# One generator per sum block, the fourth hidden tile last, pauses of the background work, and 40 cut products in a planned fp32 kernel

## The chip, the core and the metric

The kernel runs on one core of a Trainium2 chip. The metric is the device time of one execution in microseconds (us). TensorE is PE in the profile (PEld is its weight load), VectorE is DVE, ScalarE is ACT, GpSimd is POOL, and SyncE, which issues the DMAs here, is SP.

## The reference

Three stages follow each other. All arrays are float32; the weights arrive as float64 and are converted on the chip.

```python
scores = cap * tanh((q @ k.T) / sqrt(64) / cap)       # 4 batches, 12 heads, 448 x 448, head 64
attn = softmax(scores); x = attn @ v                   # x as 1792 tokens x 768
y = (sigmoid(x @ w_gate) * (x @ w_val)) @ w_out        # 768 -> 1536 -> 768
h = y @ w_in2;  out = (h * cos(h)) @ w_out2            # 768 -> 2048 -> 768
```

## The kernel before, in words

Precision: every operand of a large product is split into a high part (rounded to fp32r) and a low part (the rest), and a product is three matmuls: high x high, high x low, low x high. The rounding is an ACT cast (`wh`, `x`, `gh`, `zh`), the rest a subtraction on DVE or POOL (`wl`, `x` again, `gl`, `zl`).

The tokens are worked on in two halves of 896 (two batches). After the attention PE does, in this order: the gate and value products of half 0, done plainly (`gate_value_plain`), its result (`result(0, ...)`), the gate and value products of half 1 in pairs (`gate_value_pairs`), its result (`result(1, ...)`), and then the second block of weights, first for half 1 and then for half 0 (`cosine`). In the paired stages two output tiles of 128 rows by 896 columns are made from seven block products instead of eight: `pair_products` runs products 1, 2, 6, 5, 7, 4, 3 over KH = 3 inner tiles, 63 matmuls of 448 columns, and `pair_sums` (L827, L836) adds them up out of PSUM. The first pair of a stage goes by rows: all seven products of inner tile 0, then of 1, then of 2. The operands of the seven products are sums and differences of input blocks; `block_sums` makes them, for x1 (tile `x1r`), y1 (tile `y`) and y0. In the kernel before one generator makes them in a fixed sequence; of each block the high part is cast on L1059 and the low part is a small spawned generator on L1065.

`cosine` follows the list `cd`: C pairs (hidden tiles of w_in2) and D groups (`out_group`): C0 C1 C2 D0 C3 C4 D1 C5 C6 C7 D2 D3. A D group multiplies four hidden tiles (GRP = 4, indices kk 0 to 3) by w_out2, for two halves of 384 columns (nb) and seven token tiles t. `hidden` makes h * cos(h) of one hidden tile in seven steps over ACT and DVE (L1171, L1176, L1179, L1188, L1190, L1193 for `zh`, L1196 for `zl`).

PSUM has eight banks; a pair uses seven of them, each token tile t of a D group one until `out_evict` has copied or added it out.

What sets the order of every engine is a planner that runs when the program is built: `Order` holds one generator per activity and always emits the operation that could start earliest by its own table of costs, plus a penalty of the generator (`pen`; H_PEN for `hidden`, W_PEN for weights, S_PEN for `pair_sums`). `get` and `get_w` give buffers under limits (the W_ ranges, `room`). The engines then run their queues strictly in that order. Beside the main line the background (`bg`, `bg_loads`) converts the 32 weight units of the last stage from float64 and writes them to DRAM (`kept`), one unit for each BG_STEP of planned PE time from BG_FROM on; `bg_go` is its gate. The splits of the gated tiles (`g_split`, L945 and L948) make the operands of `result`.

`mm3` and `mm3s` emit the matmuls of one product; both have a parameter `cut`, which is 0 everywhere in the kernel before:

```python
cuts = (0, cut, S) if cut and (wi, xi) == (0, 1) else (0, S)
for s0, s1 in zip(cuts, cuts[1:]):
    nc.tensor.matmul(b.ap[:, c, s0:s1], lhsT=w.part(wi, o, P), rhs=x[xi][:, s0:s1], ...)
```

Of the kernel before, what the change touches and what calls it, by code (L numbers as in the profile page):

```python
# [14 lines left out]
P = 128  # L15
# [218 lines left out]
def softcap_attention_gated_mlp_cos_mlp(  # L234
# [14 lines left out]
    nc = tc.nc  # L249
# [7 lines left out]
    KH = KD // 2  # L257
# [9 lines left out]
    NMID, NBIG = 49, 5  # L267
    F_AHEAD = 2
    H_PEN, S_PEN = 0.4, 0.0
    LEAD, AHEAD = 99, 4  # L270
    BG_PEN, BG_RAW, BG_ROOM = 1.0, 2, 2
# [3 lines left out]
    G_SPARE = 1, 6  # L275
# [69 lines left out]
    W_A0, W_B0, W_A1, W_B1, W_CD = (7, 14), (7, 14), (14, 18), (8, 14), (12, 16)  # L345
# [249 lines left out]
    def bg_go():  # L595
        return sch.free["PE"] > BG_FROM + bg_made[0] * BG_STEP
# [147 lines left out]
    def plain_product(w, x, kks, b, first, last):  # L744
        for i, kk in enumerate(kks):
            f, l = first and i == 0, last and i == len(kks) - 1
            if x[kk] is None:
# [3 lines left out]
                lambda kk=kk, f=f, l=l: mm3(b, w, kk, x[kk], f, l),  # L751
# [24 lines left out]
    def product(i, b, c, g, X, js, last_use):  # L776
# [3 lines left out]
        for j in js:  # L780
            if not X.ready(i, j):
# [3 lines left out]
                lambda j=j: mm3s(b, c, w, o + j * P, X.part(i, j), j == 0, j == KH - 1),  # L785
# [170 lines left out]
    def gate_value_plain(hf, x, ph):  # L956
        for m in range(KF):
            wg = yield from take(ph, ("g", m))
            pg = yield from bank(2)
            yield from plain_product(wg, x, range(KD), pg, True, True)  # L960
# [39 lines left out]
    def gate_value_pairs(X):  # L1000
        for p in range(KF // 2):
            yield from pair_products(("pair", "g", p), X, False, GateSink(p), p == 0)
            yield from pair_products(("pair", "v", p), X, p == KF // 2 - 1, ValueSink(p))

    def result(hf, ph, order, sink):
        for n, m in enumerate(order):
            if n == KD - 1 and hf == 0:
                done.add("again")
            pb = yield from bank(2)
            for s in range(2):  # L1010
                w = yield from take(ph, ("o", m, s))
                for kk in range(KF // 2):
# [4 lines left out]
                    yield from plain_product(w, x, [kk], pb, i == 0, i == KF - 1)  # L1017
# [38 lines left out]
    def block_split(X, i, j, src, o, c, room):  # L1056
        t = yield from get("x", F32R, room)
        X.t[i, j] = t
        yield act(S, lambda: nc.scalar.copy(out=at(t, 0, S), in_=at(src, o, S)), [c], [t.cell("h")])  # L1059
        spawn(block_low(t, src, o, c), wpen, "blow")  # L1060

    def block_low(t, src, o, c):
# [7 lines left out]
        src.free()  # L1070

    def block_sums(X, raw, room):

        e = {}
# [11 lines left out]
        def direct(j, i):  # L1086
            r, c = {1: (raw[j], 0), 2: (raw[j + KH], 0), 3: (raw[j + KH], 1)}[i]
            yield from block_split(X, i, j, r, c * S, r.cell(c), room)
# [9 lines left out]
        def later(j, i):  # L1098
            r0, r1 = raw[j], raw[j + KH]
            if i == 7:  # L1100
                yield tt(r0, S, r1, S, r0, S, [r1.cell(1), r0.cell(1)], [r0.cell(1)])
                yield from block_split(X, 7, j, r0, S, r0.cell(1), room)
            elif i == 4:
                yield lambda: X.t[2, j].cell("l").ok
                yield tt(r1, 0, r1, 0, e[j], S, [r1.cell(0), e[j].cell(1)], [r1.cell(0)])
                e[j].free()
                yield from block_split(X, 4, j, r1, 0, r1.cell(0), room)
            else:
                o = {6: S, 5: 0}[i]
                yield from block_split(X, i, j, e[j], o, e[j].cell(o // S), room)  # L1110
# [5 lines left out]
        for j in range(KH):  # L1116
            yield from steps(j)
            yield from direct(j, 1)
# [656 lines left out]
```

## Time and profile before

| what | value |
|---|---|
| time, median of 3 runs | 1196.14 us (1195.59 to 1196.61) |
| the profiled execution | 1195.84 us, its span 1194.0 us |
| PE busy | 1159.2 us, 97% of the span |
| DVE busy | 913.1 us, 76% |
| ACT busy | 668.6 us, 56% |
| POOL busy | 258.6 us, 22% |
| mean granted TensorE clock | 0.992 |

The span is the time between the first and the last recorded instruction; 1.84 us of the profiled execution lie outside it. An engine's busy time is the time in which at least one of its instructions was on record; matmuls overlap each other in it. In us from the span's start the attention's last matmul starts at 237, the paired gate and value products run from 475 to 638, the second result follows to 733, and the paired hidden tiles and the D groups to 1190. In the rows below L715 are the matmuls of plain products, L727 those of paired products, L1255 those of the D groups.

### The profile page before, as it was taken

The numbers are of one execution on the slowest core, as the hardware profiler recorded it, in microseconds if no ns is written. First come the engines' busy times: TensorE is split into PE (matmuls) and PEld (weight loads), VectorE is DVE, ScalarE is ACT, GpSimd is POOL, SyncE is SP. The second block draws the span as 40 slices with busy tenths as digits, with TensorE's granted clock in tenths as the row PEclk, the third lists the DMA queues.
The fourth block names the chain that finished last, engine by engine and source line by source line (L and its number), as shares of the span: only waits on it lengthen the run. The fifth ranks groups of instructions, "written<-read, shape, count | busy, mean of one in ns | idle before, by whom it ended". The sixth has DMA issues, their size and how long they took to land.

```text
span 1194.0 us, 15877 instructions
## 1 busy us (share of the span) xinstructions
PE 1159.2 (97%) x6090; PEld 989.7 (83%) x6090; DVE 913.1 (76%) x1127; ACT 668.6 (56%) x785; POOL 258.6 (22%) x140
## 2 busy tenths in 40 slices
PE   8999899999999999899998999999999998999998
PEld 4444455599999999799997998899999998999998
DVE  6999999698987876787778857837578877375862
ACT  6979788865655655433346534846356256452720
POOL 3766544400011000122211000302023312011300
PEclk9999999999999999899999999999999998999999
DMA  7424244477776775323235752203025231111303
GB/s 182 113 64 97 63 122 107 131 232 257 256 255 196 229 251 185 123 101 110 93 102 182 247 172 66 80 14 93 27 69 184 82 109 35 54 53 40 93 1 93
DMA packets 126187, 148.16 MB, mean 124 GB/s; under 512 B 49952, under 2 KB 98976, under 8 KB 126112
## 3 DMA queue, kind: packets, MB, share of 16 engines
q1 hardware_dynamic: 125824, 147.09, 39.9%
q8 instruction: 48, 0.79, 0.3%
q14 instruction: 27, 0.22, 0.1%
q10 hardware_dynamic: 288, 0.07, 0.0%
HBM read 112.13 MB, written 35.00 MB: 123 GB/s over the span
## 4 chain that ended last, share of the span: by engine, by line
PE 88%; DVE 7%; ACT 2%; issue 1%; SPq 0%; DMA 0%; DVEq 0%; ACTq 0%
PE pt L727 30%; PE pt L715 28%; PE pt L1255 19%; PE pt L1420 5%; PE pt L1395 4%; DVE r L1614 1%; ACT p L1486 1%; PE pt L1374 1%; PE pt L1441 1%; ACT p L1503 1%; DVE sum L1593 1%; DVE gl L948 1%; DVE zl L1196 1%; DVE h L827 0%; SPq L1329 0%
## 5 line engine op out<-in xcount | busy, mean ns | idle before, releaser
L727 PE MATMUL pt<-x,wh 128*128 128x448 f32 x1260 | 344.6, 369 | 7.1 <-DVE x L1065 3.7
L727 PEld LDWEIGHTS pt<-x,wh 128*128 128x128 f32 x1260 | 237.7, 189 | 31.5 <-DVE x L1065 4.4
L727 PE MATMUL pt<-x,wl 128*128 128x448 f32 x504 | 185.7, 368 | 0.0
L490 ACT CAST wh<-f 128x768 fp32r<-128x768 f32 (+1 forms) x164 | 122.9, 776 | 92.6 <-DVE f L655 50.3
L501 POOL TENSOR_TENSOR wl<-f,wh 128x768 fp32r<-128x768 f32 x41 | 80.1, 1957 | 381.8 <-ACT wh L490 297.3
L1255 PE MATMUL pt<-wh,zh 128*128 128x384 f32 x448 | 151.7, 339 | 6.1 <-ACT zh L1193 6.1
L1255 PE MATMUL pt<-wh,zl 128*128 128x384 f32 x448 | 151.9, 339 | 2.3 <-DVE zl L1196 2.3
L1255 PE MATMUL pt<-wl,zh 128*128 128x384 f32 x448 | 151.2, 337 | 0.0
L501 DVE TENSOR_TENSOR wl<-f,wh 128x768 fp32r<-128x768 f32 x95 | 96.8, 1024 | 45.9 <-ACT wh L490 45.6
L1486 ACT ACTIVATE p<-pt,tanh_scale 112x896 f32<-112x896 f32 x96 | 92.6, 1008 | 37.3 <-PE pt L1395 35.6
L727 PEld LDWEIGHTS pt<-x,wl 128*128 128x128 f32 x504 | 95.0, 188 | 9.3
L1278 DVE TENSOR_TENSOR acc<-pt,acc 128x384 f32<-128x384 f32 x84 | 46.6, 555 | 65.0 <-PE pt L1255 64.3
L1255 PEld LDWEIGHTS pt<-wh,zh 128*128 128x128 f32 x448 | 85.5, 191 | 6.8 <-ACT zh L1193 6.7
L1255 PEld LDWEIGHTS pt<-wh,zl 128*128 128x128 f32 x448 | 85.3, 190 | 3.8 <-DVE zl L1196 3.8
L1503 ACT ACTIVATE p<-p,cap_sb 112x1792 f32<-112x1792 f32 x48 | 86.2, 1795 | 0.0
L1255 PEld LDWEIGHTS pt<-wl,zh 128*128 128x128 f32 x448 | 85.4, 191 | 0.1
L715 PE MATMUL pt<-gl,wh 128*128 128x448 f32 x276 | 79.4, 369 | 4.1 <-DVE gl L948 4.1
L715 PE MATMUL pt<-xh,wh 128*128 128x448 f32 x288 | 83.4, 371 | 0.0
L715 PE MATMUL pt<-xl,wh 128*128 128x448 f32 x288 | 81.8, 365 | 0.0
L715 PE MATMUL pt<-xh,wl 128*128 128x448 f32 x288 | 81.8, 365 | 0.0
L1420 PE MATMUL pt<-p,v 112*64 112x448 f32 x384 | 77.5, 545 | 4.2 <-ACT p L1486 4.2
L1395 PEld LDWEIGHTS pt<-qs,ks 64*112 64x112 f32 x576 | 46.2, 171 | 41.9 <-ACT p L1486 16.7
(121 smaller groups left out, 2075.3 us busy)
## 6 DMA issues: line engine op xcount, KB each, us to landing
f<-kept SPq DMA_DIRECT2D x100, 384.0 KB, 3.5
kept<-f SPq DMA_DIRECT2D x36, 384.0 KB, 3.4
braw<-in_moe_w_in_dram SPq DMA_DIRECT2D x16, 768.0 KB, 5.5
kept<-bf SPq DMA_DIRECT2D x32, 384.0 KB, 2.7
braw<-in_moe_w_out_dram SPq DMA_DIRECT2D x16, 768.0 KB, 6.1
raw<-in_moe_w_gate_dram SPq DMA_DIRECT2D x12, 768.0 KB, 5.1
raw<-in_moe_w_val_dram SPq DMA_DIRECT2D x12, 768.0 KB, 5.9
raw<-in_moe_w_out_dram SPq DMA_DIRECT2D x12, 768.0 KB, 5.4
```

What stands on the lines that cost most here:

```text
L490: yield act(n, lambda: nc.scalar.copy(out=at(h, 0, n), in_=at(src, o, n)), sc, [h.cell("h")])
L501: lambda e: e.tensor_tensor(out=w.part(1, 0, n), in0=at(src, o, n), in1=w.part(0, 0, n).bitcast(F32), op=ALU.subtract),
L715: nc.tensor.matmul(b.ap[:, c, s0:s1], lhsT=w.part(wi, kk * P, P), rhs=x.part(xi, c * S + s0, s1 - s0), start=(first and (wi, xi) == (0, 0) ...
L727: nc.tensor.matmul(b.ap[:, c, s0:s1], lhsT=w.part(wi, o, P), rhs=x[xi][:, s0:s1], start=(first and (wi, xi) == (0, 0)), stop=(last and (wi ...
L948: lambda e: e.tensor_tensor(out=at(l, lo, n), in0=at(b), in1=f32(h, 0, n), op=ALU.subtract),
L1196: lambda e: e.tensor_tensor(out=at(zl), in0=uv, in1=f32(zh), op=ALU.subtract),
L1255: nc.tensor.matmul(b.ap[:, 0, :NB], lhsT=at(z[zi], t * P, P), rhs=w.part(wi, k * NB, NB), start=(first and (zi, wi) == (0, 0)), stop=(last ...
L1278: lambda: nc.vector.tensor_tensor(out=o, in0=ps(b, 0, NB), in1=o, op=ALU.add),
L1395: nc.tensor.matmul(ps(b, h)[:CP], lhsT=at(ks, ki * S + c * CP, CP)[r], rhs=at(qs, qi * S, S)[r], start=(n_ == 0), stop=(n_ == 2),)
L1420: nc.tensor.matmul(ps(b)[h * D : (h + 1) * D], lhsT=tv[:CP, h, c, :], rhs=at(p, (2 * j + h) * S, S)[:CP], start=(c == 0), stop=(c == NC - 1),)
L1486: lambda: nc.scalar.activation(out=two(at(p, 2 * j * S, 2 * S))[:CP], in_=both(b)[:CP], func=AF.Tanh, scale=tanh_scale[:CP],),
L1503: lambda: nc.scalar.activation(out=pv, in_=pv, func=AF.Exp, scale=cap_sb[:CP]),
```

## The change

All 40 cut products are made by the parameter `cut` of `mm3` and `mm3s`: in the middle matmul of a product (high weights, low operand) the 448 columns are done as one matmul of 256 and one of 192 with the same weights, loaded again. There are 6 in the first gate products (every second gate tile), 6 in the results (the first product of every second output tile) and 28 in the paired stages (the first inner tile of product 1 of every pair: 12 gate and value pairs, 16 hidden pairs).

`block_sums` spawns one generator for each block, with its own penalty, after its sum is made; a generator casts and then subtracts. In the first half (nb = 0) of D0 the D group runs kk 0 to 2 for all seven token tiles and then kk 3 for all seven. The background loads pause while "entry" is set: from the last output tile of a result (the last but one of half 1) to the second pair of the following stage (to C2 in `cosine`), and in the last gate and value pair. Penalties and buffer limits get other numbers.

```diff
@@ -265,14 +265,16 @@
     NMID, NBIG = 49, 5
+    CUT = 256
     F_AHEAD = 2
-    H_PEN, S_PEN = 0.4, 0.0
+    X_PEN, X_STEP = 0.3, 0.0
+    H_PEN, S_PEN, H_STEP = -0.25, 0.2, 0.0
     LEAD, AHEAD = 99, 4
-    BG_PEN, BG_RAW, BG_ROOM = 1.0, 2, 2
+    BG_PEN, BG_RAW, BG_ROOM = 1.0, 2, 1
     BG_FROM, BG_STEP = 240.0, 15.5
...
     ATT_PEN, A_PEN = 0.0, 1.0
-    G_SPARE = 1, 6
+    G_SPARE = (1, 4)
@@ -342,7 +344,7 @@
-    W_A0, W_B0, W_A1, W_B1, W_CD = (7, 14), (7, 14), (14, 18), (8, 14), (12, 16)
+    W_A0, W_B0, W_A1, W_B1, W_CD = (7, 14), (9, 14), (14, 16), (7, 12), (12, 18)
     w_live = [0]
@@ -593,7 +595,7 @@
     def bg_go():
-        return sch.free["PE"] > BG_FROM + bg_made[0] * BG_STEP
+        return "entry" not in done and sch.free["PE"] > BG_FROM + bg_made[0] * BG_STEP
@@ -741,14 +743,14 @@
-    def plain_product(w, x, kks, b, first, last):
+    def plain_product(w, x, kks, b, first, last, cut=0):
         for i, kk in enumerate(kks):
...
                 6 * MM448,
-                lambda kk=kk, f=f, l=l: mm3(b, w, kk, x[kk], f, l),
+                lambda kk=kk, f=f, l=l: mm3(b, w, kk, x[kk], f, l, cut if f else 0),
                 w.cells() + x[kk].cells(),
@@ -782,7 +784,7 @@
                 3 * MM448,
-                lambda j=j: mm3s(b, c, w, o + j * P, X.part(i, j), j == 0, j == KH - 1),
+                lambda j=j: mm3s(b, c, w, o + j * P, X.part(i, j), j == 0, j == KH - 1, CUT if (i, j) == (1, 0) else 0),
                 [*w.cells(), *X.cells(i, j)],
@@ -957,7 +959,7 @@
             pg = yield from bank(2)
-            yield from plain_product(wg, x, range(KD), pg, True, True)
+            yield from plain_product(wg, x, range(KD), pg, True, True, CUT if m % 2 else 0)
             wg.free()
@@ -999,11 +1001,17 @@
         for p in range(KF // 2):
+            if p == 1:
+                done.discard("entry")
+            if p == KF // 2 - 1:
+                done.add("entry")
             yield from pair_products(("pair", "g", p), X, False, GateSink(p), p == 0)
...
         for n, m in enumerate(order):
+            if n == KD - 1 - hf:
+                done.add("entry")
             if n == KD - 1 and hf == 0:
@@ -1014,7 +1022,7 @@
                     x = {kk: G[hf, i]}
-                    yield from plain_product(w, x, [kk], pb, i == 0, i == KF - 1)
+                    yield from plain_product(w, x, [kk], pb, i == 0, i == KF - 1, CUT if n % 2 == 0 else 0)
                     if n == KD - 1:
@@ -1053,13 +1061,10 @@
-    def block_split(X, i, j, src, o, c, room):
+    def block_split(X, i, j, src, o, c, room, low_done):
         t = yield from get("x", F32R, room)
+        yield act(S, lambda: nc.scalar.copy(out=at(t, 0, S), in_=at(src, o, S)), [c], [t.cell("h")])
         X.t[i, j] = t
-        yield act(S, lambda: nc.scalar.copy(out=at(t, 0, S), in_=at(src, o, S)), [c], [t.cell("h")])
-        spawn(block_low(t, src, o, c), wpen, "blow")
-
-    def block_low(t, src, o, c):
         yield either(
@@ -1068,10 +1073,11 @@
         src.free()
+        low_done.add((i, j))
...
-        e = {}
+        e, low_done = {}, set()
@@ -1085,7 +1091,7 @@
             r, c = {1: (raw[j], 0), 2: (raw[j + KH], 0), 3: (raw[j + KH], 1)}[i]
-            yield from block_split(X, i, j, r, c * S, r.cell(c), room)
+            yield from block_split(X, i, j, r, c * S, r.cell(c), room, low_done)
@@ -1099,15 +1105,16 @@
                 yield tt(r0, S, r1, S, r0, S, [r1.cell(1), r0.cell(1)], [r0.cell(1)])
-                yield from block_split(X, 7, j, r0, S, r0.cell(1), room)
+                src, o = r0, S
             elif i == 4:
-                yield lambda: X.t[2, j].cell("l").ok
+                if not (2, j) in low_done:
+                    yield lambda: (2, j) in low_done
                 yield tt(r1, 0, r1, 0, e[j], S, [r1.cell(0), e[j].cell(1)], [r1.cell(0)])
                 e[j].free()
-                yield from block_split(X, 4, j, r1, 0, r1.cell(0), room)
+                src, o = r1, 0
             else:
-                o = {6: S, 5: 0}[i]
-                yield from block_split(X, i, j, e[j], o, e[j].cell(o // S), room)
+                src, o = e[j], {6: S, 5: 0}[i]
+            spawn(block_split(X, i, j, src, o, src.cell(o // S), room, low_done), X_PEN + X_STEP * j, "x")
@@ -1115,12 +1122,12 @@
             yield from steps(j)
-            yield from direct(j, 1)
-            yield from direct(j, 2)
+            for i in (1, 2):
+                spawn(direct(j, i), X_PEN + X_STEP * j, "x")
             yield from first_sums(j)
...
                 yield from later(j, i)
-            yield from direct(j, 3)
+            spawn(direct(j, 3), X_PEN + X_STEP * j, "x")
@@ -1135,7 +1142,7 @@
         def done(self, i):
-            spawn(hidden(self.hf, 2 * self.p + i, self.h[i]), H_PEN, "hidden")
+            spawn(hidden(self.hf, 2 * self.p + i, self.h[i]), H_PEN + H_STEP * ((2 * self.p + i) % GRP), "hidden")
@@ -1240,8 +1247,12 @@
+            late = GRP - 1 if gi == 0 and nb == 0 else 0
+            for t in range(NTT if late else 0):
+                for kk in range(late):
+                    yield from part(t, kk)
             for t in range(NTT):
-                for kk in range(GRP):
+                for kk in range(late, GRP):
                     yield from part(t, kk)
@@ -1299,6 +1310,8 @@
             last = i == KF2 // 2 - 1
+            if i == 2:
+                done.discard("entry")
             yield from pair_products(("pair", "i", i), X, last, HiddenSink(hf, i), i == 0)
@@ -1701,6 +1714,7 @@
         done.add(("A", 1))
+        done.discard("entry")
         Y1 = Blocks()
```

Three places show what this does to the order. First DVE at the entry to the paired gate and value products, third inner tile of x1: `t475` and `t470` are its two sums so far, `x1r181` and `x1r220` its two raw blocks (L1079 is a sum, L1065 a low part, L827 a sum out of PSUM, L655 and L501 weights, L431 to L447 background). Before:

```order
L1079 TENSOR_TENSOR x1r181_1431<-x1r220_1708,x1r181_1431 128x448
L439 TENSOR_SCALAR bf457_3890<-bf457_3890 128x768
L1065 TENSOR_TENSOR x491_4111<-x1r181_1431,x491_4111 128x448
L655 TENSOR_TENSOR f466_3935<-f463_3916,f466_3935 128x384
L501 TENSOR_TENSOR wl494_4127<-e489_4076,wh493_4125 128x768
L827 TENSOR_TENSOR sg495_4134<-pt_69,part492_4120 128x896
L827 TENSOR_TENSOR part492_4120<-pt_69,sg495_4134 128x896
L655 TENSOR_TENSOR f463_3916<-f463_3916,e489_4076 128x384
L1079 TENSOR_TENSOR x1r220_1708<-x1r220_1708,t475_4001 128x448
L447 SCALAR_TENSOR_TENSOR bf457_3890<-braw456_3857,bf457_3890 128x768
L501 TENSOR_TENSOR wh498_4148<-f463_3916,wh498_4148 128x384
L1065 TENSOR_TENSOR x499_4150<-x1r220_1708,x499_4150 128x448
```

And now (L1085 is the sum, L1070 the low part, L829 the sum out of PSUM):

```order
L657 TENSOR_TENSOR e489_4087<-e489_4087,f459_3914 128x384
L433 TENSOR_SCALAR bf454_3890<-bf454_3890 128x768
L1085 TENSOR_TENSOR x1r181_1431<-x1r220_1708,x1r181_1431 128x448
L1085 TENSOR_TENSOR x1r220_1708<-x1r220_1708,t470_3990 128x448
L1070 TENSOR_TENSOR x490_4116<-x1r181_1431,x490_4116 128x448
L1070 TENSOR_TENSOR x492_4126<-x1r220_1708,x492_4126 128x448
L1070 TENSOR_TENSOR x491_4125<-x1r220_1708,x491_4125 128x448
L657 TENSOR_TENSOR f461_3918<-f459_3914,f461_3918 128x384
L829 TENSOR_TENSOR sg495_4143<-pt_69,part493_4132 128x896
L829 TENSOR_TENSOR part493_4132<-pt_69,sg495_4143 128x896
```

The last sum, which writes `x1r220` (`x1r220_1708`), stood behind two sums out of PSUM, which wait for PE, and now stands ahead of them, as do the three low parts of this tile.

Second DVE at the first D group, where the hidden tiles of pair C1 (`u809` and `u807` before, `u808` and `u806` now) meet the sums out of PSUM of pair C2 (`h815`, `h818`; now `h812`). Before:

```order
L1190 TENSOR_TENSOR u786_6161<-h777_6117,u786_6161 128x896
L827 TENSOR_TENSOR h815_6313<-pt_69,part811_6284 128x896
L1179 SCALAR_TENSOR_TENSOR u807_6271<-u807_6271 128x896
L1196 TENSOR_TENSOR zl812_6286<-u788_6163,zh789_6164 128x896
L827 TENSOR_TENSOR part811_6284<-pt_69,h815_6313 128x896
L827 TENSOR_TENSOR h818_6355<-pt_69,part811_6284 128x896
L1190 TENSOR_TENSOR u809_6273<-h802_6248,u809_6273 128x896
L827 TENSOR_TENSOR h815_6313<-pt_69,part811_6284 128x448
L1190 TENSOR_TENSOR u807_6271<-h794_6199,u807_6271 128x896
L501 TENSOR_TENSOR wl822_6376<-f805_6260,wh821_6370 128x768
L1179 SCALAR_TENSOR_TENSOR u825_6379<-u825_6379 128x896
L1196 TENSOR_TENSOR zl820_6366<-u809_6273,zh810_6274 128x896
```

And now:

```order
L1186 SCALAR_TENSOR_TENSOR u808_6296<-u808_6296 128x896
L1186 SCALAR_TENSOR_TENSOR u806_6294<-u806_6294 128x896
L1197 TENSOR_TENSOR u808_6296<-h797_6255,u808_6296 128x896
L1197 TENSOR_TENSOR u806_6294<-h789_6206,u806_6294 128x896
L1203 TENSOR_TENSOR zl814_6343<-u808_6296,zh809_6297 128x896
L1203 TENSOR_TENSOR zl815_6351<-u806_6294,zh807_6295 128x896
L829 TENSOR_TENSOR h812_6328<-pt_69,part805_6292 128x896
L829 TENSOR_TENSOR part805_6292<-pt_69,h812_6328 128x896
L829 TENSOR_TENSOR h820_6392<-pt_69,part805_6292 128x896
L829 TENSOR_TENSOR h812_6328<-pt_69,part805_6292 128x448
```

The six steps of the two hidden tiles stood among the four sums of the next pair and ended with `zl820` and `zl827`; now all six stand ahead of the four sums.

Third the splits of the gated tiles at the start of the second result: DVE before (L948 is a split, L431 to L455 a background conversion, L904 the product of gate and value):

```order
L904 TENSOR_TENSOR sg644_5182<-val669_5301,sg644_5182 128x896
L904 TENSOR_TENSOR sg638_5139<-val657_5248,sg638_5139 128x896
L501 TENSOR_TENSOR wl671_5313<-f666_5280,wh668_5297 128x768
L439 TENSOR_SCALAR bf652_5218<-bf652_5218 128x768
L948 TENSOR_TENSOR gl663_5273<-sg526_4321,gh662_5272 128x896
L447 SCALAR_TENSOR_TENSOR bf652_5218<-braw620_5005,bf652_5218 128x768
L948 TENSOR_TENSOR gl674_5338<-sg532_4365,gh673_5337 128x896
L455 SCALAR_TENSOR_TENSOR bf652_5218<-bf652_5218,braw620_5005 128x768
L948 TENSOR_TENSOR gl676_5349<-sg554_4526,gh675_5348 128x896
L431 TENSOR_SCALAR bf678_5359<-bf678_5359 128x768
L948 TENSOR_TENSOR gl680_5365<-sg560_4571,gh679_5364 128x896
```

And POOL now (L950 is a split, L503 a weight):

```order
L503 TENSOR_TENSOR wl627_5075<-f604_4899,wh626_5073 128x768
L503 TENSOR_TENSOR wl632_5106<-f617_4993,wh629_5086 128x768
L950 TENSOR_TENSOR g637_5149<-sg499_4163,g637_5149 128x896
L503 TENSOR_TENSOR wh642_5188<-f617_4993,wh642_5188 128x384
L503 TENSOR_TENSOR wl649_5223<-f644_5195,wh648_5212 128x768
L950 TENSOR_TENSOR gl655_5259<-sg524_4326,gh654_5258 128x896
L950 TENSOR_TENSOR gl663_5291<-sg531_4372,gh662_5290 128x896
L503 TENSOR_TENSOR wl670_5327<-f660_5274,wh665_5296 128x768
```

Of the twelve splits POOL had one and DVE eleven before; now POOL has `gl655` and `gl663` besides, and DVE the remaining eight, which still alternate with background operations there.

## Rows read from the trace of the kernel before

**Rows 1.** Page, busy time of TensorE, us (share of span) and instructions

```profile
PE 1159.2 (97%) x6090; PEld 989.7 (83%) x6090; DVE 913.1 (76%) x1127; ACT 668.6 (56%) x785; POOL 258.6 (22%) x140
```

**Rows 2.** Windows, TensorE: stretch, length, busy us (matmuls), clock, DMA

```profile
300.00:400.00 100.00, 100.00 (x495) 1.00 0.72 232
489.00:496.00 7.00, 4.48 (x11) 0.51 0.01 2
500.00:600.00 100.00, 100.00 (x485) 1.00 0.31 103
660.00:740.00 80.00, 80.00 (x396) 1.00 0.49 163
```

**Rows 3.** Chain of waits: start us, length us, engine, matmul line, count

```profile
492.26 146.17 PE pt L727 x698
...
864.63 39.05 PE pt L727 x189
...
1131.68 58.26 PE pt L1255 x336
```

**Rows 4.** Timeline, weight loads after a wait: start, length, line, [idle before <-releaser]

```profile
643.47 0.30 PEld L715 LDWEIGHTS pt<-gl,wh 128*128 128x128 f32 x2 [2.54 <-DVE gl L948]
...
644.18 0.19 PEld L715 LDWEIGHTS pt<-gh,wh 128*128 128x128 f32 x1
```

**Rows 5.** Timeline, TensorE, entry to the paired gate products

```profile
486.18 0.37 PE L727 MATMUL pt<-x,wl 128*128 128x448 f32 x1
489.99 0.74 PE L727 MATMUL pt<-x,wh 128*128 128x448 f32 x1 [3.44 <-ACT x L1059]
492.26 0.74 PE L727 MATMUL pt<-x,wh 128*128 128x448 f32 x1 [1.54 <-DVE x L1065]
...
496.07 0.37 PE L727 MATMUL pt<-x,wl 128*128 128x448 f32 x1
```

**Rows 6.** Timeline, DVE, the same stretch

```profile
480.47 0.62 DVE L1079 TENSOR_TENSOR x1r<-x1r,x1r 128x448 f32<-128x448 f32 x1
...
485.44 1.09 DVE L827 TENSOR_TENSOR sg<-pt,part 128x896 f32<-128x896 f32 x1 [1.76 <-ACT wh L490]
...
488.10 0.62 DVE L1079 TENSOR_TENSOR x1r<-x1r,t 128x448 f32<-128x448 f32 x1
```

**Rows 7.** Timeline, TensorE, start of the second result

```profile
640.74 0.57 PE L715 MATMUL pt<-gh,wh 128*128 128x448 f32 x2
643.47 0.67 PE L715 MATMUL pt<-gl,wh 128*128 128x448 f32 x2 [2.16 <-DVE gl L948]
...
658.71 0.67 PE L715 MATMUL pt<-gl,wh 128*128 128x448 f32 x2 [0.39 <-DVE gl L948]
```

**Rows 8.** Timeline, DVE, the same stretch

```profile
642.33 1.08 DVE L948 TENSOR_TENSOR gl<-sg,gh 128x896 fp32r<-128x896 f32 x1
643.34 0.95 DVE L447 SCALAR_TENSOR_TENSOR bf<-braw,bf 128x768 int32<-128x768 int32 x1
```

**Rows 9.** Timeline, TensorE, entry to the paired hidden tiles

```profile
746.73 0.47 PE L727 MATMUL pt<-x,wh 128*128 128x448 f32 x1 [2.15 <-DVE x L1065]
```

**Rows 10.** Timeline, TensorE, first D group of half 1

```profile
774.27 0.34 PE L1255 MATMUL pt<-wh,zl 128*128 128x384 f32 x1
777.66 0.45 PE L1255 MATMUL pt<-wh,zh 128*128 128x384 f32 x1 [3.05 <-ACT zh L1193]
...
782.68 0.34 PE L1255 MATMUL pt<-wh,zh 128*128 128x384 f32 x1
```

**Rows 11.** Timeline, DVE, the same stretch

```profile
771.76 1.09 DVE L827 TENSOR_TENSOR h<-pt,part 128x896 f32<-128x896 f32 x1 [0.73 <-PE pt L727]
772.77 1.08 DVE L1190 TENSOR_TENSOR u<-h,u 128x896 f32<-128x896 f32 x1
```

**Rows 12.** Timeline, TensorE, first D group of half 0

```profile
1001.69 0.34 PE L1255 MATMUL pt<-wh,zl 128*128 128x384 f32 x1
...
1011.36 0.35 PE L1255 MATMUL pt<-wl,zh 128*128 128x384 f32 x1
```

## The prediction

> **What bounds the kernel now.** I read the page first. TensorE is busy for 1159.2 us of a span of 1194.0 us [rows 1], so no other engine can be the bound on average: only some 35 us of idle time, the speed of single matmuls, and the clock can be won. The windows show the speed. In a hundred microseconds without a gap and at full clock TensorE started 495 matmuls of 448 columns, in another hundred, just as full and at the same clock, 485, and later again 396 in eighty [rows 2]. That is 202.0, 206.2 and 202.0 ns for one. So there are two paces, 4.2 ns apart, and the busy share hides it. The chain of waits shows where the slow one holds: 39.05 us for 189 matmuls of paired products are 206.6 ns, while 384 columns take 58.26 / 336 = 173.4 ns [rows 3]. I looked for what stands at the changes of pace. The slow pace starts after the clock has been at half (489 to 496, granted clock 0.51 [rows 2]), and again in the pairs that follow a D group; the fast pace returns at the second result [rows 7], where TensorE stopped for an operand and the next matmul had to wait for its own weight load.
>
> Then the timelines around each gap, TensorE beside the engine that ended it. The gaps have one form: TensorE reaches an operand whose last step stands in DVE's queue behind something that itself waits for TensorE.
>
> **The change part by part.** I count the excess of a place from start to start, less the matmuls in between at their pace, so that half clock after a gap is in it.
>
> *Entry to the paired gate products.* From 486.18 to 496.07, 9.89 us, there start 12 matmuls [rows 5]; at 203 ns they need 2.4 us, so the excess is 7.4 us. The late operands are blocks 4 and 3 of the third inner tile. Their sum started at 488.10, because it stood behind sums out of PSUM of which the first started at 485.44; the sum before it had started at 480.47 [rows 6]. In the new order the last sum follows directly: two sums and three low parts at 0.6 us each and one cast on ACT before the first low part, about 3.6 us, so ready at about 484.1. TensorE wants them from 486.4 on. I take the whole 7.4 us; at worst half stays.
>
> *Start of the second result.* From 640.74 to 658.71, 17.97 us, there are 56 matmuls, 11.4 us, so 6.6 us excess [rows 7]. DVE gives one split per 1.0 us and then does a background step [rows 8]; from 643.47 to 658.71 the nine tiles came every 1.69 us [rows 7], while TensorE uses one up in six matmuls, 1.22 us. The new order moves two splits to POOL and ahead, but leaves eight on DVE, with the background steps still between them. The first of the eight stands where the one of 642.33 stood [rows 8] and is the fifth tile, wanted two tiles after 640.74, at 643.2, so it is just in time; each of the next seven is 0.47 us too slow, 3.3 us. I take 3.3 us as won (6.6 less 3.3), with bounds of 0 and 6.6.
>
> *Entry to the paired hidden tiles.* The same form, an idle time of 2.15 us [rows 9]. All eleven steps of the third tile of y now stand together, ahead of the first sum out of PSUM. I take 2.1 us.
>
> *First D group of each half.* 774.27 to 782.68 holds 13 matmuls: 8.41 less 2.25 is 6.2 us [rows 10]. 1001.69 to 1011.36 holds 17: 9.67 less 2.95 is 6.7 us [rows 12]. The product h * cos(h) of the third hidden tile started at 772.77, behind a sum that had to wait for TensorE until 771.76 [rows 11]. Now six steps of 1.0 us stand ahead of those sums. Their inputs leave PSUM one pair earlier, 12.8 us before the corresponding sum at 771.76 and one more 2 us later, so by about 761. As an estimate seven steps of one tile after each other, ACT's taken at DVE's 1.0 us, and two of the other tile make 9 us: 770, against a start of the group shortly before 774. Besides, the fourth tile is asked for only after 63 matmuls, 10.9 us. What is late next are the sums of pair C2, by some 4 us; their three adjacent banks are not asked for until the group is over, and the group's seven banks come one per 1.6 us. I take 12.7 of the 12.9 us. The price would be a late bank, 0 to 4 us, taken as 0.
>
> *Pauses of the background.* The last two conversions move behind the first D group. They hold large buffers that the group's accumulators want; the last accumulator is wanted some 11 us after the group's start, and the first conversion's last step stands in DVE's queue just behind the hidden tiles of C2, about as late. The evictions hide it, so I cost it at nothing; without that cover it is four steps like the one of 643.34 [rows 8], 3.8 us, once.
>
> *The cuts.* The trace has no matmul of 256 or 192 columns. By the difference of 202.0 and 173.4 ns over 64 columns, 0.45 ns each, 256 columns cost 116 ns. For 192 the next weight load counts: two loads in a row took 0.30 us, one alone 0.19 [rows 4], so loads follow each other in 0.11 us and 192 columns, at 0.45 ns, are over earlier. A cut product then takes 226 ns, 24 more than a whole one, 1.0 us for 40. Below: the columns alone, 0. Above: each piece as slow as 384 columns, 347 ns, 5.8 us. I take 1.0, since the load is the nearest row. What the cut does besides: the matmul after the short piece waits for its own load, the very state after which the fast pace came back at the second result. So I expect each cut to set the fast pace.
>
> The Trainium skill ("TensorE: Matmul & The Clock Gate", section "Back-to-back issue gap") says that a warm matmul of N columns follows the one before in N/2.4 + 2.5 ns. That is 189 ns for 448 columns; both paces here are slower, and it has no second pace. By it the two pieces would take 192 ns, so the cuts would cost 0.1 us in all, and there would be no pace to win back; that result stands below as a rival.
>
> *Pace.* Slow today are 698 matmuls of the paired gate and value stage [rows 3] and 13 hidden pairs of 63, 819, that follow a D group: 1517 x 4.2 ns = 6.4 us. The 698 (2.9 us) lose the cause, the half clock, even without cuts; the 819 (3.4 us) rest on the cuts.
>
> Sum: 7.4 + 3.3 + 2.1 + 12.7 + 6.4 - 1.0 = 30.9 us. The profiled execution took 1195.84 us (1.84 outside its span), so 1164.9; the median of the runs lies 0.3 above it, so 1165.
>
> **Rivals.**
> *The pace does not come back by a cut.* For it: nobody sees in the trace why there are two paces, and I argue from what stood before a change of pace. Against it: after the restart at 643, at full clock, the fast pace followed and held from 660 to 740 [rows 2, 7]. The 819 stay slow: 1165 + 3.4 = 1168.5. If a cut even sets the slow pace, the 698 stay slow too (2.9), and so do the fast stretches of today, 237 to 486 and 660 to 774, 363 us or 1800 matmuls (7.5): 1179.
> *The waits come back in part.* For it: at the second result they do by my own count, and orders that were planned with other durations than the chip's gave the gaps of today. Against it: the new orders have 2 us or more to spare. If half of the 25.5 us of the five places stays, with its half clock, 1178.
> *Slower: pair sums too late for PSUM.* Six hidden steps now stand ahead of the next pair's sums in all 16 hidden pairs. A pair lasts 63 x 203 ns = 12.8 us; its three adjacent banks are filled by its sixth product at about 11 us and wanted again at 12.8 + 5.5 = 18.3, so the sums have about 6 us to spare. The steps alone are 6.0 us, less the 1 or 2 that stood there already. If ACT's part stretches them to 9 us, TensorE waits 3 us in 15 pairs, 45 us: 1210. It decides from 8.3 us on. Against it: my count gives 4 us.
>
> **How the numbers follow.** Forecast 0.60, no pace 0.18, half of the waits 0.18, late sums 0.04. The forecast's own range is 1160 (the second result without any wait, cuts for nothing) to 1169. To hold eight in ten the range goes up to 1178, where the bad ends of both milder rivals lie. About 0.2%, 2.4 us, is what a measurement can tell from no change. Faster by more: 0.94, since all three milder cases are; within: 0.02, for a mixture with late sums; slower: 0.04.
>
> **What would show it.** Right: no idle time over 0.3 us of TensorE at 486, 744, 774 and 1002, and no granted clock under 1 between the attention and the end; at the second result waits for `gl` of 0.3 to 0.6 us each, 3 us in all; 493 to 495 matmuls of 448 columns per 100 us, also in the pairs behind D groups. Wrong: 485 there, a cut product over 250 ns, or TensorE waiting for the release of a bank in a hidden pair.

## The result, and the profile after

The changed kernel takes 1167.64 us (median of 4 runs, 1167.36 to 1170.85) against 1196.38 us of the kernel before on the same chip: ratio 0.976, 95% interval 0.974 to 0.978. The forecast was 1165. The profiled execution took 1167.75 us, its span 1165.7 us, 28.3 less than before.

Below, L717 are the matmuls of plain products, L729 those of paired products, L1266 those of the D groups. The page's first part, busy us (share) and instructions, answers to [rows 1]:

```profile
PE 1148.2 (99%) x6130; PEld 986.6 (85%) x6130; DVE 923.3 (79%) x1120; ACT 670.2 (57%) x785; POOL 270.9 (23%) x147
```

The 40 more matmuls are the cuts. TensorE does the same work in 11 us less busy time: pace and half clock, which [rows 1] hid. Windows of TensorE (stretch, length, busy us and matmuls, clock, DMA) answer to [rows 2], with two more:

```profile
300.00:400.00 100.00, 100.00 (x495) 1.00 0.71 231
489.00:496.00 7.00, 7.00 (x37) 1.00 0.61 198
500.00:600.00 100.00, 100.00 (x499) 1.00 0.33 107
660.00:740.00 80.00, 80.00 (x398) 1.00 0.35 114
318.00:342.00 24.00, 24.00 (x118) 1.00 0.78 262
350.00:374.00 24.00, 24.00 (x121) 1.00 0.68 215
```

The half clock at 489 is gone. The counts of the long windows now contain cut pieces and hide what the last two rows show: within the gate products, fast throughout before, a slow stretch lies beside a fast one. From start to start the two paces are 206.7 and 202.7 ns. The chain of waits (start, length, line, count) answers to [rows 3]:

```profile
476.20 147.20 PE pt L729 x732
...
844.62 38.40 PE pt L729 x192
...
1103.24 58.28 PE pt L1266 x336
```

Three pairs behind a D group take 38.40 us with their three cuts, 39.05 before. The view of waits of TensorE (line <- engine, tile and line waited for: us, times, longest) has, besides the attention's waits, only

```profile
PE pt L717 <- DVE gl L950: 1.3, 4, 0.4
PE pt L1266 <- DVE zl L1203: 1.0, 1, 1.0
```

The timelines at the places of [rows 5], [rows 9] and [rows 10] have no wait left; at that of [rows 12] one row has:

```profile
982.07 0.45 PE L1266 MATMUL pt<-wh,zl 128*128 128x384 f32 x1 [0.97 <-DVE zl L1203]
```

The second result, where [rows 7] and [rows 8] stood, first TensorE, then DVE:

```profile
638.05 0.67 PE L717 MATMUL pt<-gl,wh 128*128 128x448 f32 x2 [0.38 <-DVE gl L950]
...
647.67 0.67 PE L717 MATMUL pt<-gl,wh 128*128 128x448 f32 x2
```

```profile
635.04 1.08 DVE L950 TENSOR_TENSOR gl<-sg,gh 128x896 fp32r<-128x896 f32 x1
636.04 0.95 DVE L457 SCALAR_TENSOR_TENSOR bf<-bf,braw 128x768 int32<-128x768 int32 x1
636.91 1.08 DVE L950 TENSOR_TENSOR gl<-sg,gh 128x896 fp32r<-128x896 f32 x1
637.91 0.55 DVE L433 TENSOR_SCALAR bf<-bf 128x768 f32<-128x768 f32 x1
638.38 1.08 DVE L950 TENSOR_TENSOR gl<-sg,gh 128x896 fp32r<-128x896 f32 x1
```

Eight splits still alternate with background steps, 1.47 or 1.87 us from one to the next, against 1.22 us in which TensorE uses one up.

The best reading is by stage, from the first matmul of a stage to the first of the next (us, from the matmul records; "no cuts" and "best" are the experiments e1_no_cuts and e9_split_pause below):

| stage | before | after | no cuts | best |
|---|---|---|---|---|
| gate, value, result of half 0 | 237.23 | 238.62 | 237.23 | 237.23 |
| paired gate and value | 163.43 | 154.47 | 153.37 | 153.37 |
| second result | 94.33 | 91.42 | 90.12 | 87.55 |
| C0 to C2, half 1 | 40.80 | 38.64 | 38.30 | 38.30 |
| D0, half 1 | 35.31 | 29.15 | 29.15 | 29.15 |
| the 13 pairs behind D groups | 169.21 | 166.38 | 169.21 | 166.16 |
| D0, half 0 | 35.89 | 30.41 | 29.89 | 30.49 |
| D1, both halves | 59.48 | 58.30 | 58.25 | 58.30 |

Executions of one kernel differ by some 3 us more, because the attention, where the change has a single cut, ends at 237 us in some and at 240 in others (e2, e3, e5, e7, e10 and e11 were profiled with the late end). So stages are compared, and a difference of single times below 3 us is not read.

### The profile page after: what moved, and what is told of

Read it like the earlier page. It is cut to its first block, busy times and chain, and to the rows that moved or that the text cites. A ratio compares the mean times of both kernels' runs of the same rounds, so it can differ in the third digit from the quotient of the medians.

```text
span 1165.7 us, 15996 instructions
## 1 busy us (share of the span) xinstructions
PE 1148.2 (99%) x6130; PEld 986.6 (85%) x6130; DVE 923.3 (79%) x1120; ACT 670.2 (57%) x785; POOL 270.9 (23%) x147
## 4 chain that ended last, share of the span: by engine, by line
PE 88%; DVE 7%; ACT 3%; issue 1%; SPq 0%; DMA 0%; DVEq 0%; ACTq 0%
PE pt L717 29%; PE pt L729 28%; PE pt L1266 20%; PE pt L1433 5%; PE pt L1408 4%; DVE r L1627 2%; ACT p L1499 1%; PE pt L1387 1%; PE pt L1454 1%; ACT p L1516 1%; DVE sum L1606 1%; SPq L1342 0%; DVE h L829 0%; DVE u L1197 0%; DVE gl L950 0%
## 5 line engine op out<-in xcount | busy, mean ns | idle before, releaser
L729 PE MATMUL pt<-x,wh 128*128 128x448 f32 (+2 forms) x1288 | 339.1, 361 | 0.0
L729 PEld LDWEIGHTS pt<-x,wh 128*128 128x128 f32 x1288 | 241.9, 188 | 19.4
L729 PE MATMUL pt<-x,wl 128*128 128x448 f32 x504 | 185.2, 367 | 0.0
L503 POOL TENSOR_TENSOR wl<-f,wh 128x768 fp32r<-128x768 f32 x46 | 95.3, 2074 | 319.3 <-ACT wh L492 311.7
L1266 PE MATMUL pt<-wh,zl 128*128 128x384 f32 x448 | 149.8, 334 | 1.0 <-DVE zl L1203 1.0
L1266 PE MATMUL pt<-wl,zh 128*128 128x384 f32 x448 | 149.7, 334 | 0.0
L1266 PE MATMUL pt<-wh,zh 128*128 128x384 f32 x448 | 149.7, 334 | 0.0
L503 DVE TENSOR_TENSOR wl<-f,wh 128x768 fp32r<-128x768 f32 x90 | 93.9, 1048 | 34.9 <-ACT wh L492 34.6
L729 PEld LDWEIGHTS pt<-x,wl 128*128 128x128 f32 x504 | 94.7, 188 | 7.6 <-DVE wl L503 0.2
L1266 PEld LDWEIGHTS pt<-wh,zl 128*128 128x128 f32 x448 | 84.1, 188 | 1.3 <-DVE zl L1203 1.3
L1266 PEld LDWEIGHTS pt<-wh,zh 128*128 128x128 f32 x448 | 84.1, 188 | 0.1
L1266 PEld LDWEIGHTS pt<-wl,zh 128*128 128x128 f32 x448 | 84.1, 188 | 0.1
L717 PE MATMUL pt<-xh,wh 128*128 128x448 f32 x288 | 83.5, 371 | 0.0
L717 PE MATMUL pt<-xl,wh 128*128 128x448 f32 (+2 forms) x294 | 82.2, 362 | 0.0
L717 PE MATMUL pt<-xh,wl 128*128 128x448 f32 x288 | 82.0, 366 | 0.0
L1627 DVE RECIPROCAL r<-pt 128x448 f32<-128x448 f32 x24 | 70.8, 2949 | 9.3 <-PE pt L1454 9.3
```

The costliest lines, as they stand in the source:

```text
L503: lambda e: e.tensor_tensor(out=w.part(1, 0, n), in0=at(src, o, n), in1=w.part(0, 0, n).bitcast(F32), op=ALU.subtract),
L717: nc.tensor.matmul(b.ap[:, c, s0:s1], lhsT=w.part(wi, kk * P, P), rhs=x.part(xi, c * S + s0, s1 - s0), start=(first and (wi, xi) == (0, 0) ...
L1266: nc.tensor.matmul(b.ap[:, 0, :NB], lhsT=at(z[zi], t * P, P), rhs=w.part(wi, k * NB, NB), start=(first and (zi, wi) == (0, 0)), stop=(last ...
L1627: [("DVE", 2.95, False, lambda: nc.vector.reciprocal(out=at(r, 0, S), in_=ps(den)), 0.0)],
```

## The experiments

Theory A is the prediction's: every cut sets the fast pace. Theory B came from the changed trace: a D group leaves the slow pace, a cut behind it sets the fast one, but a cut made in the fast pace can set the slow one. Each was run against the kernel before on its chip.

**e1_no_cuts.**

```diff
-    CUT = 256
+    CUT = 0
```

> The changed kernel with no cut at all; the order of every engine stays as it is. Theory A (the prediction: each cut sets the fast pace): the 819 matmuls in pairs behind D groups go back to 206.7 ns (+3.3), the 40 cuts' cost goes (-1.3), the first paired stage stays fast: 1167.6 + 2.0 = 1169.6. Theory B (read from the changed kernel's trace: a cut moves TensorE on through four states of which one is slow, a D group and some restarts leave it slow): +3.3 behind D groups, -1.3 for the cuts, -1.9 for some 480 matmuls of slow stretches between 237 and 640 us that become fast, and +1.5 where the restart at the second result leaves the slow pace with no cut to end it: 1169.2, with no slow matmul between 237 and 630 us and only slow ones from the restart to the first D group. Rival C (the pace has nothing to do with cuts, the new order alone made the pairs behind D groups fast): those stay at 202.7 ns, 1166.3 or less.

1165.76 us (6 runs, 1165.56 to 1168.48), ratio 0.974 [0.971, 0.977]. The chain:

```profile
237.36 237.32 PE pt L717 x1170
474.68 153.38 PE pt L729 x756
...
840.78 39.05 PE pt L729 x189
```

Not one slow matmul of 448 columns from the attention to the first D group, and only slow ones behind D groups. So rival C falls, and A in its size: without cuts the kernel is not 2.0 us slower; its profiled span is 2.0 us shorter, its median 1.9. The restart at the second result left the fast pace here, B had expected the slow one.

**e2_cuts_only.** The kernel before with `cut` passed on as in the change, and nothing else.

> The kernel before with the 40 cuts and nothing else of the change. Theory A: all 1517 slow matmuls become fast, -6.1, cuts +1.3: 1191.5. Theory B: 819 behind D groups become fast (-3.3), of the 698 of the first paired stage some 500 (-2.0), cuts +1.3, and some 290 matmuls of the gate products become slow (+1.2): 1193.6, with slow stretches of one cut's length in about one cut of four wherever no D group lies between cuts. Rival C: no pace changes, +1.3: 1197.7. The waits (30.6 us of idle time) stay as before in all three.

1195.83 us (12 runs), ratio 0.999 [0.997, 1.001]. In the chain the stretch with its first 8 cuts after the attention is 1.4 us longer (237.32 before), two parts of it at the slow pace, and the pairs behind D groups gain as in the changed kernel:

```profile
240.60 238.72 PE pt L716 x1178
...
869.24 38.40 PE pt L728 x192
```

After the attention the profiled execution is 1.4 us shorter than that of before (954.98 against 956.42 us from the first gate product to the end), too little for the times to show. By their own terms A had expected 4.8 less, B 2.8; C falls by the second row.

**e3_few_cuts.** Six cuts instead of 40.

```diff
-  plain_product(wg, x, range(KD), pg, True, True, CUT if m % 2 else 0)
+  plain_product(wg, x, range(KD), pg, True, True)
-  ... CUT if n % 2 == 0 else 0)
+  ... CUT if (hf, n) == (1, 2) else 0)
+        prev = "C" if hf else "D"
+            cut, prev = CUT if prev == "D" else 0, kind
-            yield from pair_products(..., HiddenSink(hf, i), i == 0)
+            yield from pair_products(..., HiddenSink(hf, i), i == 0, cut)
```

> The changed kernel with 6 cuts instead of 40: in the first pair behind each of the five D groups that a pair follows, and in the third output tile of the second result. Theory A: as the changed kernel less 34 cuts of 33 ns, 1166.5. Theory B: also no slow stretch but the one from the restart to the cut in the second result: -1.1 for the cuts, -2.2 for some 550 slow matmuls: 1164.3, with 202.7 ns everywhere else. Rival C: as the kernel without cuts, plus 0.2.

1166.52 us (5 runs, 1164.85 to 1168.30). The one cut that was not behind a D group did the harm: the second result ran fast after its restart, and from the cut at 663 us on every matmul was slow until D0, 206.7 ns each in the second row, while the five others set the fast pace:

```profile
644.55 78.14 PE pt L717 x377
722.69 39.06 PE pt L729 x189
...
845.59 38.34 PE pt L729 x190
```

That is the plainest contradiction of A: the same edit in the fast pace sets the slow one.

**e8_five_cuts.** As e3 without the cut in the second result.

> The changed kernel with 5 cuts instead of 40: only in the first pair behind each D group that a pair follows. Theory B (a D group leaves the slow pace, one cut behind it sets the fast one, which holds until the next D group; elsewhere the pace is fast already and a cut can only cost its 33 ns or set the slow pace): every stretch of 448 columns after the attention at 202.7 ns, 13 pairs each 0.22 us shorter than in the kernel without cuts: its 1165.8 less 2.8 is 1163.0. Theory A of the prediction (every cut sets the fast pace, none ends it): the same 1163.0, but then the 40 cuts of the changed kernel should have cost no more than 35 x 0.033 = 1.2 over this one, 1164.2, where 1167.6 was measured. Rival C (the pace behind a D group is set by something in the D group that varies from run to run): some of the five stretches stay at 206.7.

1166.22 us (4 runs, 1165.74 to 1168.29), not 1163.0. The pairs behind D groups gained as expected (38.34), but this time the restart at the second result left the slow pace:

```profile
237.72 237.32 PE pt L717 x1170
...
641.55 78.43 PE pt L717 x376
719.98 39.06 PE pt L729 x189
```

Up to there its orders are those of e1_no_cuts, where the same 376 matmuls took 76.98 us. So a stop of TensorE leaves one pace or the other, and the order does not fix which: 1.45 us in the second result and 0.76 in C0 to C2.

**e9_split_pause.** e8 and a pause of the background's conversions at the splits:

```diff
         done.add(("A", 1))
-        done.discard("entry")
 ...
+            if n == 1:
+                done.discard("entry")
 ...
-            yield lambda: len(bg_raw) > 0
+            yield lambda: len(bg_raw) > 0 and "entry" not in done
```

> As the kernel with five cuts, and the background conversions (not only their loads) pause from the last gate and value pair until the second output tile of the second result, so that the eight splits of gated tiles on DVE stand next to each other instead of alternating with background steps. The prediction's mechanism (those splits come 0.25 to 0.65 us late each because a background step of 0.55 to 0.95 us stands between two of them): a split each 1.1 us against 1.22 us of six matmuls, so of the 2.5 us excess at the start of the second result at most 0.5 us at its first tile stays: 2.0 less than with five cuts, 1161.0. Rival (the tiles come as fast as ACT casts them and as buffers come free; the steps between only fill the gaps): the gaps stay, 1163.0; or the background comes too late for the first pairs of the last stage and TensorE waits there: over 1165.

1160.58 us (4 runs, 1160.41 to 1163.61), ratio 0.969 [0.966, 0.972], 7 us below the changed kernel. Seven splits now stand together on DVE (first row, its timeline), and TensorE never waits there (the chain):

```profile
630.47 7.10 DVE L950 TENSOR_TENSOR gl<-sg,gh 128x896 fp32r<-128x896 f32 x7
```

```profile
627.89 87.55 PE pt L717 x432
715.44 38.30 PE pt L729 x189
```

87.55 us are 432 matmuls at 202.7 ns: with the wait its restart went too, and with that the draw between the paces. The prediction's account of what remains there is confirmed by taking its cause away; in size it was 2.6 us (90.12 without cuts, where the restart was fast, less 87.55), not 3.3.

**e4_late0.** `late = 0` in `out_group`.

> The changed kernel with the fourth hidden tile not last in the first half of D0: every token tile takes its four hidden tiles in order again. Theory of the prediction (the late order carries part of the 12.7 us won at the first D groups): the fourth tile is wanted 9 matmuls after the group's start, TensorE waits some 2 to 6 us at each half, 1171 to 1178. Rival (read from the changed trace: the steps of the hidden tiles ahead of the next pair's sums do it alone; all four tiles are ready by 761 at half 1 and by 982 at half 0): no wait at half 1, about the same 1 us at half 0: 1167.6 to 1168.

1169.23 us (6 runs, 1166.60 to 1170.98); profiled span 1164.5. D0 took 29.15 and 30.41 us, to the hundredth as with the late order, and the one wait is the same:

```profile
PE pt L1266 <- DVE zl L1203: 1.0, 1, 1.0
```

The late fourth tile is worth nothing; the rival is right.

**e5_old_prio.** `H_PEN, S_PEN = 0.4, 0.0`, the late order kept.

> The changed kernel with the old penalties of the hidden tiles and the pair sums (0.4 and 0.0); the fourth tile still comes last in the first half of D0. Theory (the steps of the hidden tiles standing ahead of the next pair's sums do all of the 12.7 us at the first D groups, the late order nothing): the third tile's product stands behind sums that wait for TensorE again, 4 to 6 us with half clock at each half: 1176 to 1180. Rival (the late order does its part): the group reaches the fourth tile only after 63 matmuls, at most 1 to 2 us at each half for the third: 1169 to 1171.

1184.65 us (4 runs, 1182.38 to 1185.89), 17 more than the changed kernel; in the profiled executions 15.6 of it lie behind the attention. D0 took 37.87 and 36.26 us, more than before the change. The waits:

```profile
PE pt L1266 <- ACT zh L1200: 8.1, 2, 5.0
...
PE pt L1266 <- DVE zl L1203: 1.8, 2, 1.4
```

The penalties of the hidden tiles and of the pair sums, changed together here, do all of it.

**e6_old_sums.** The old `block_sums` and `block_split`.

> The changed kernel with the old block sums (one fixed sequence, high parts cast in it, low parts spawned). In the order that results, one sum out of PSUM stands ahead of the last two sums of the third inner tile of x1, none ahead of those of y1. Theory of the prediction (what stands behind a sum out of PSUM is late by that sum's own wait for TensorE): a wait at the entry to the paired gate products returns, 3 to 7.4 us with its half clock, none at the entry to the hidden tiles: 1171 to 1175. Rival (the pauses of the background and the other limits removed that wait): no wait, 1167.6.

1179.39 us (4 runs, 1177.46 to 1180.62). The paired gate and value stage took 164.29 us, 9.8 more than in the changed kernel, and as much as before the change; C0 to C2 stayed at 38.64. It is not the expected mechanism, though. The sum out of PSUM ahead of the last two sums waited for nothing (first row); in the fixed sequence these two simply stand later, at 491.12 and 493.25 (482.60 and 483.13 in the changed kernel), and the first took 2.21 us instead of 0.62 beside a POOL step (see the last section):

```profile
489.02 1.08 DVE L829 TENSOR_TENSOR sg<-pt,part 128x896 f32<-128x896 f32 x1
...
491.12 2.21 DVE L1087 TENSOR_TENSOR x1r<-x1r,x1r 128x448 f32<-128x448 f32 x1
```

D0 of half 1 took 33.09 us because its order changed too: three sums of the next pair stand ahead of the last steps of the hidden tiles again (last row of the waits):

```profile
PE pt L729 <- ACT x L1067: 5.7, 2, 4.6
...
PE pt L1267 <- DVE zl L1204: 1.5, 2, 0.9
PE pt L1267 <- ACT zh L1201: 1.3, 1, 1.3
```

**e7_no_pause.** `bg_go` without "entry".

> The changed kernel without the pauses of the background. The prediction costs them at nothing: background steps then stand among the last steps of the third inner tiles and ahead of the first D group, but evictions and the weight splits hide them: 1167.6, no new wait over 1 us. Rival (the steps push the block sums behind the first sum out of PSUM or hold the buffers of the D group's accumulators): a wait of 2 to 4 us at the entry to the hidden tiles or in the first half of D0, 1170 to 1174.

1170.56 us (4 runs, 1169.79 to 1172.18). D0 of half 1 took 30.58 us, 1.4 more, the second result 0.4 more; the entry to the hidden tiles stayed free:

```profile
PE pt L1266 <- DVE zl L1203: 1.5, 2, 1.0
PE pt L1266 <- ACT zh L1200: 0.4, 1, 0.4
```

So the pauses are worth about 1.8 us, between the two expectations; the rest of the difference is the late end of the attention.

**e10_cut224** and **e11_cut384.** e9 with `CUT = 224`, and with `CUT = 384`, one run of each.

> The kernel with five cuts and the pause at the splits, cut into 224 and 224 columns instead of 256 and 192. Theory (behind a D group the matmul that waits for its own weight load behind a short piece sets the fast pace, whatever the piece's length): all five stretches at 202.7 ns, the time unchanged at 1160.5. Rival (the pace depends on where the cut's time leaves the queue, so on the size): one or more of the stretches at 206.7, 0.5 to 0.75 us for each.

> The same with pieces of 384 and 64 columns. The pieces take longer together (174 + 90 ns and some 28 ns at the next matmul, about 90 ns over a whole one, 0.4 us for five). Theory as for 224 columns: the five stretches at 202.7 ns, 1160.8. Rival: some or all of them at 206.7, up to 3.3 us more: 1164.

1164.14 and 1163.81 us, both with the late end of the attention. Behind every D group the pace is fast with either size; first the chain of 224 columns, then that of 384:

```profile
840.94 38.31 PE pt L729 x190
```

```profile
840.84 38.39 PE pt L729 x190
```

189 whole matmuls take 38.30 (e9, C0 to C2), so a cut costs 0.01 us with 224 columns, 0.04 with 256 and 0.09 with 384.

**e12_low_on_dve.** e9, and in `low`, once the second result is done:

```diff
+        late = ("B", 1) in done
+        yield dve(n, lambda: fn(nc.vector), r, c) if late else either(n, fn, r, c, LOW_BIAS)
```

> The kernel with five cuts and the pause at the splits, where the low parts of the weights are made by DVE alone after the second result (35 steps of 0.95 us more on DVE, none of 1.85 to 2.1 us on POOL). Theory (the 2.74 us of the low part that TensorE waits for in the first half of D0 of half 0 is its own 1.08 us behind POOL's subtraction of 1.85 us that started 0.05 us before it; a DVE step with both operands in SBUF does not run beside one of POOL): that step takes 1.1 us, the wait of 1.0 us goes: 1159.3. Rival 1 (the 2.74 us has another reason): the step stays long. Rival 2 (DVE then is late elsewhere, 35 us more work in 440 us): new waits, 1161 to 1165.

1163.31 us (4 runs, 1161.79 to 1164.97). Inconclusive: the planner put the low part in question on POOL instead, and TensorE waits for it there (rival 2):

```profile
PE pt L1265 <- POOL zl L1202: 1.7, 2, 1.4
```

## Why the prediction was right, and the step that failed

**Entry to the paired gate products (7.4) and the 698 matmuls of its stage (2.9).** Right in size: the order alone takes the stage from 163.43 to 153.37 us, 10.1 against 10.3 forecast, and e6 brings the wait back. In e1 the fast pace held there without a stop and without a cut. In mechanism the late last sum is right, but the second wait of [rows 5], 1.54 us, had another cause that the count did not see: the first low part behind that sum took 2.23 us instead of 0.62 beside a POOL step that had begun at 489.54 (see the last section; two low parts in one row):

```profile
489.98 2.77 DVE L1065 TENSOR_TENSOR x<-x1r,x 128x448 fp32r<-128x448 f32 x2
```

**Second result (3.3).** 94.33 to 91.42, 2.9; without cuts 4.2. What was left is shown by e9. How much is seen depends on the pace that the restart happens to leave: with the same 40 cuts e4 took 90.20 us there.

**Entry to the paired hidden tiles (2.1).** 40.80 to 38.64, 2.2. No run brought this wait back (e5, e6 and e7 stayed within 0.02 us of 38.64), so which part of the change removed it is not shown.

**First D groups (12.7).** 11.6 won, by the priorities alone (e4, e5). One of the prediction's own signs, no idle time over 0.3 us at 1002, failed here. What stays is one low part on DVE that takes 2.74 us at 978.27 (two take 3.74 together, one 1.08):

```profile
978.27 3.74 DVE L1203 TENSOR_TENSOR zl<-u,zh 128x896 fp32r<-128x896 f32 x2
```

**Late pair sums (the rival at 1210).** Did not come: no wait for a bank in a hidden pair.

**Pauses (0).** Mis-sized: about 1.8 us (e7). Not in the sum at all: the two D1 groups, 59.48 to 58.25 without cuts, 1.2 us.

**The failing step: "So I expect each cut to set the fast pace", and with it the 3.4 us for the 819 matmuls net of the cuts' 1.0.** Two terms were nearly right: behind D groups the pairs gain 169.21 - 166.38 = 2.8 us with their cuts, and a cut costs 0.03 to 0.04 us, not 0.024 (its pieces start 118 and 90 ns apart, and the next matmul comes some 28 ns late). What was missing is the 27 cuts elsewhere. I had argued from one restart after which the fast pace came back, and called it the state that makes it; the same state led to the slow pace in e8. In the changed kernel, six of the 27 cuts made in the fast pace after the attention set the slow one, which held until the next cut: at 314, 446, 502, 553, 605 and 722 us, some 540 matmuls, and from the restart another 75. After minus e1, by the first seven rows of the table: +1.4, +1.1, +1.3, +0.3, 0, -2.8, +0.5, together +2.0 us with D1 and the start of the products, where the step gave -2.4. Not all of it is pace: the +1.3 hangs on the restart, and the +0.5 is a longer wait for the low part above, at which TensorE arrives earlier. That the sum nevertheless came within 2.6 us of the time is in part luck: the order gave 30.3 us without a cut against 28.4 forecast, and this hid nearly half of the 4.4 us by which the step was out. The rival "the pace does not come back by a cut", with 1168.5, names the failing step but has the wrong place: the pace did come back behind D groups. Its worse half, "if a cut even sets the slow pace" (1179), has the places, the gate products and paired gate products, but takes every cut for what six did.

Which cuts do harm can be read from the matmul records. In the slow pace every gap from start to start is 206 or 207 ns. The fast pace is a rhythm of five gaps: one of 199 or 200 ns, one of 206 or 207, and three of 202 or 203. In the seven kernels with cuts outside the first pair behind a D group (the changed kernel and e2 to e7), leaving out cuts in the attention and beside a D group, a gap or the half clock:

| the cut is made | cuts | slow pace after it |
|---|---|---|
| fast pace, right behind the gap of 199 or 200 ns | 39 | 39 |
| fast pace, anywhere else | 125 | 0 |
| slow pace | 38 | 0 |

So the place in the rhythm told the outcome of all 202 cuts; in the pairs the bad place came round every fourth cut (502, 553 and 605 us above). No run moved a cut by one matmul to test this, and why there are two paces and why the rhythm has this effect stays open.

## What to carry to other kernels

An operand's last step that stands behind a step which itself waits for TensorE is worth looking for at the start of each stage: two priorities (e5) and one generator per block (e6) carried over two thirds of the gain, and pausing the background for eight steps gave more again. A trick that repairs a pace belongs only where the trace shows the bad pace: behind D groups 5 cuts do what 40 did, and the other 35 cost time. Compare stages, not totals, when single runs scatter by more than the effect.

## What the runs showed of the hardware

A matmul of 448 columns ran at 202.7 or at 206.7 ns from start to start, at full clock and without a gap, for as long as 237 us (fast, e1) or 142 us (slow, [rows 3] from 496 on) on end; after a D group of 384 columns always at 206.7 (ten of ten stretches without cuts, five each in e1 and before the change), after a stop of TensorE at either.

The low part of 2.74 us above began 0.05 us after a POOL step of the weights:

```profile
978.22 1.85 POOL L503 TENSOR_TENSOR wl<-f,wh 128x768 fp32r<-128x768 f32 x1 [0.33 <-ACT wh L492]
```

What was left of it, 1.80 us, and the 1.08 of a low part make 2.88, nearly the 2.74. In the changed trace 64 pair sums, which read PSUM, overlapped a POOL step and none took over 1.10 us. Steps of DVE that read SBUF alone did take longer: after the attention 32 of them began under a POOL step with over 0.2 us left, and 31 took their usual time plus what was left, less 0.13 to 0.14 us (left 0.34, 0.66, 1.10 and 1.79 us: 0.75 instead of 0.55, 1.15 instead of 0.62, 2.04 instead of 1.08, 2.60 instead of 0.95). The one exception began within 0.02 us of POOL's. Three of the 31 read a single operand (TENSOR_SCALAR). So such a step waits for POOL's to end, as the records show; e12 does not test it, since it moved the step away. The Trainium skill ("SBUF — State Buffer", section "SBUF: two separate sides") says the same: a VectorE operation with two SBUF inputs and a GpSimd operation that reads SBUF exclude each other, and whichever starts second waits.
